# Hash bits of keys and queries from one four-column-group product set, and mask products over 32 rows

## The chip, the cores and the metric

The kernel runs on one core of one Trainium2 chip. The metric is device time in microseconds from the start to the end of one execution; several executions are timed and the median stands for the kernel. The engines are TensorE (PE; its weight loads are listed apart as PEld), VectorE (DVE), ScalarE (ACT), GpSimd (POOL) and SyncE (SP), which issues most DMAs. Each runs its own instructions in order and waits for the others by semaphores.

## What is computed

The reference is attention over 16 heads (2 batches of 8) of 768 tokens and 64 features, and behind it a gated layer and a layer of eight experts, which the change does not touch. What matters here is the mask of the attention: a query and a key see each other only when the signs of their six projections agree.

```
q_bits = (np.einsum('bhsd,dk->bhsk', q, proj) > 0).astype(np.int64)
k_bits = (np.einsum('bhsd,dk->bhsk', k, proj) > 0).astype(np.int64)
q_bucket = np.sum(q_bits * powers, axis=-1)
k_bucket = np.sum(k_bits * powers, axis=-1)
mask = q_bucket[:, :, :, None] == k_bucket[:, :, None, :]
scores = scale * np.matmul(q, k.transpose(0, 1, 3, 2))
scores = np.where(mask, scores, -1000000000.0)
attn = exp(scores - max); attn /= sum;  out = attn @ v
```

## The kernel before

**Pairs and units.** The 16 heads are taken as eight pairs. Of a pair i, the keys and queries are transposed by TensorE into `K[i]` and `Q[i]`: 64 features of one head in partitions 0 to 63, of the other in 64 to 127, with 768 tokens side by side. `QS` and `KS` are copies with the partition halves swapped, made by DMA. The attention runs over 48 units u, six for each pair; a unit is 256 queries of one head.

**Scores.** `scores(u, t)` with t = 0, 1 makes the scores of 128 queries against all 768 keys, in two PSUM banks of 384 keys (n = 0, 1). Two float32 products (line 270), one from the rows 0 to 63 and one from the rows 64 to 127, run side by side, each in two passes; then two bfloat16 products (line 273) add the mask to the same banks. For them `KF` holds the key's sign bits times 2^60, so that the maximum of a row is large only where all six bits agree, and a masked score vanishes in the exponential. The mask products read 64 rows at the same two places of the array as the score products; 7 bits of each head stand in 32 rows.

**Hash bits.** `lz` holds the projection as a weight block of 64 columns for a half. `signs(i, 0)` multiplies it with the two halves of `Q[i]` in two column groups of 64 (line 233), `signs(i, 1)` does so for `K[i]` (line 246). In the next unit ACT takes the signs of each (line 227, once for `QF`, once for `sk`), SP issues two DMAs that copy `QF` with its partition halves exchanged to `QG` (line 240), and `masks` multiplies `sk` twice into `KF` (line 216). `opening` does the same for the first pair, in smaller pieces.

**Order of the work.** The loop over u at the end of `attention` sets the order on every engine. On TensorE an iteration holds the scores (u + 1, 0), the scores (u + 1, 1), and then one of three things: half of the values' product `pv` of an earlier head (line 320, 96 passes on array tiles of 32 rows and 64 columns), or, in one of three iterations, a piece of a later pair: its transposes (`turned`, line 114) and its `signs` by turns, six iterations apart for each. DVE takes the row maxima (`nm`, line 278) and turns the exponentials in 32 by 32 blocks (`et`, line 308), ACT makes the exponentials (`e`, line 284) and copies `pv` out (lines 340), POOL normalises (line 301). The scores have two PSUM buffers of two banks, so the scores (u + 1, t) wait until the exponential of (u, t) has been read. `signs` and `turned` write the banks `pvb` that `pv` uses, so they wait for the copies on ACT, and the `pv` behind them waits for ACT to have read theirs. `hook` inserts pieces of weight conversion, and from unit 41 on the first products of the gated layer (line 597), at places fixed when the program is written.

Of the kernel before, what the change touches and what calls it, by code (L numbers as in the profile page):

```python
# [25 lines left out]
class Kernel:  # L26
# [8 lines left out]
    def constants(self, const):  # L35
        nc = self.nc
        NB, D = self.proj.shape[1], self.D
        self.ident = const.tile([128, 128], F32, name="ident")
        make_identity(nc, self.ident)

        p = const.tile([128, 2], I32, name="p")
        nc.gpsimd.iota(p[:, 0:1], pattern=[[0, 1]], base=0, channel_multiplier=1)
        nc.vector.tensor_scalar(p[:, 1:2], p[:, 0:1], 5, 1, ALU.logical_shift_right, ALU.bitwise_and)
        nc.vector.tensor_scalar(p[:, 0:1], p[:, 0:1], 31, None, ALU.bitwise_and)
        pf = const.tile([128, 2], F32, name="pf")
        nc.vector.tensor_copy(pf, p)
        bit = const.tile([128, 2], F32, name="bit")
        nc.vector.tensor_scalar(bit[:, 0:1], pf[:, 0:1], float(NB), None, ALU.is_lt)  # L50
        nc.vector.tensor_scalar(bit[:, 1:2], pf[:, 0:1], float(NB), None, ALU.is_equal)
        self.bias = const.tile([128, 1], F32, name="bias")
        nc.vector.scalar_tensor_tensor(self.bias, bit[:, 0:1], -1e-9, bit[:, 1:2], ALU.mult, ALU.add)
        fac = self.fac = const.tile([128, 2], F32, name="fac")
        nc.vector.tensor_scalar(fac[:, 0:1], bit[:, 1:2], -float(NB) * BIG, None, ALU.mult)
        nc.vector.scalar_tensor_tensor(fac[:, 0:1], bit[:, 0:1], BIG, fac[:, 0:1], ALU.mult, ALU.add)
        nc.vector.tensor_tensor(fac[:, 1:2], fac[:, 0:1], pf[:, 1:2], ALU.mult)
        nc.vector.tensor_tensor(fac[:, 0:1], fac[:, 0:1], fac[:, 1:2], ALU.subtract)
        self.lz = const.tile([128, 2, 2, 32], F32, name="lz")
        nc.gpsimd.memset(self.lz, 0.0)  # L60
        self.pr = const.tile([128, NB], F32, name="pr")
        const.tile([128, 72], F32, name="pad")

    def attention(self, xh, xl, pools, hook):
        nc = self.nc
        sb, ps_s, ps_pv = pools
        NB = self.proj.shape[1]
        S, D = self.S, self.D
        NC = S // 128
# [3 lines left out]
        H2 = S // 2  # L73
        for tag, shape, dt, n in (
            ("et", [128, NC * S], F32, 2), ("e", [128, 2 * S], F32, 3), ("vr", [128, NC * 256], F32, 2), ("raw", [128, 2 * S], F32, 1),
            ("q", [128, S], F32, 2), ("qs", [128, S], F32, 2), ("k", [128, S], F32, 2), ("ks", [128, H2], F32, 2),
            ("xp", [128, S], F32, 2), ("co", [128, S], F32, 2), ("qf", [128, H2], BF16, 2), ("qg", [128, H2], BF16, 2), ("kf", [128, S], BF16, 2), ("sk", [128, H2], BF16, 1),
        ):
            sb.tile(shape, dt, tag=tag, name=tag, bufs=n)
        raw, Q, QS, K, KS, QF, QG, KF, VR = {}, {}, {}, {}, {}, {}, {}, {}, {}  # L80

        def load(i, qs=(nc.sync, nc.sync)):
            b, hp = pairs[i]
# [15 lines left out]
        pvb = [ps_pv.tile([128, 2, 512], F32, tag=f"pv{n}", name="pv") for n in range(2)]  # L99
# [37 lines left out]
        def opening():  # L137
# [3 lines left out]
            lz = self.lz.rearrange("p a b c -> p (a b c)")  # L141
            for t, tag, n in ((Q, "q", S), (QS, "qs", S), (K, "k", S), (KS, "ks", H2)):
                t[0] = sb.tile([128, n], F32, tag=tag, name=tag, bufs=2)
            for t, tag in ((QF, "qf"), (QG, "qg")):
                t[0] = sb.tile([128, H2], BF16, tag=tag, name=tag, bufs=2)
# [19 lines left out]
            def sign(dst, src):  # L165
                nc.scalar.activation(dst, src, AF.Sign, bias=self.bias[:src.shape[0]], scale=2.0 ** 100)
# [15 lines left out]
            out(Q[0][:, queries], pvb[0][:, 1, :H2])  # L182
            for c in range(3, NC):
                first(pvb[1], 0, c)
            for x, r in enumerate(half):
                nc.tensor.matmul(
                    pvb[1][r, 0, :H2], lz[:, r], K[0][:, x * H2:(x + 1) * H2], start=True, stop=True, tile_position=(0, 64 * x)
                )
            sign(sk, pvb[1][:, 0, :H2])
            nc.tensor.matmul(pvb[0][:, 0, :H2], lz, Q[0][:, keys], start=True, stop=True)  # L190
            for x in range(2):
                sign((QF, QG)[x][0][half[x]], pvb[0][half[x], 0, :H2])
            for j in range(2):
                nc.vector.tensor_scalar(KF[0][:, j], sk, self.fac[:, j:j + 1], None, ALU.mult)
# [4 lines left out]
            def rest():  # L199
                nc.tensor.matmul(pvb[0][:, 1, :H2], lz, Q[0][:, queries], start=True, stop=True)  # L200

                def out(*_):
                    for x in range(2):
                        sign((QF, QG)[1 - x][0][half[x]], pvb[0][half[x], 1, :H2])

                return out

# [2 lines left out]
        later = []  # L210

        def masks(eng=nc.scalar):
            for kf, sk in later:
                for j in range(2):
                    if eng is nc.scalar:
                        eng.mul(kf[:, j], sk, self.fac[:, j:j + 1])
                    else:
                        eng.tensor_scalar(kf[:, j], sk, self.fac[:, j:j + 1], None, ALU.mult)
            later.clear()

        def signs(i, n):
            p = pvb[n]
            lz = self.lz.rearrange("p a b c -> p (a b c)")
            half = [slice(64 * x, 64 * x + 64) for x in range(2)]

            def sign(dst, src):
                nc.scalar.activation(dst, src, AF.Sign, bias=self.bias[:src.shape[0]], scale=2.0 ** 100)

            if n == 0:
                QF[i] = sb.tile([128, H2], BF16, tag="qf", name="qf", bufs=2)  # L230
                QG[i] = sb.tile([128, H2], BF16, tag="qg", name="qg", bufs=2)
                for x, r in enumerate(half):
                    nc.tensor.matmul(
                        p[r, 0, :H2], lz[:, r], Q[i][:, x * H2:(x + 1) * H2], start=True, stop=True, tile_position=(0, 64 * x)
                    )

                def out(*_):
                    sign(QF[i], p[:, 0, :H2])
                    for x in range(2):
                        nc.sync.dma_start(out=QG[i][half[1 - x]], in_=QF[i][half[x]])  # L240

                return out
            KF[i] = sb.tile([128, 2, H2], BF16, tag="kf", name="kf", bufs=2)
            sk = sb.tile([128, H2], BF16, tag="sk", name="sk", bufs=1)
            for x, r in enumerate(half):
                nc.tensor.matmul(
                    p[r, 0, :H2], lz[:, r], K[i][:, x * H2:(x + 1) * H2], start=True, stop=True, tile_position=(0, 64 * x)
                )

            def out(*_):  # L250
                sign(sk, p[:, 0, :H2])
                later.append((KF[i], sk))

            return out
# [7 lines left out]
        def scores(u, t):  # L262
            i, j, g = units[u]
            c = 2 * g + t
            st = ST[u, t] = ps_s.tile([128, 2, 512], F32, tag="s", name="st")
            ql = slice(c * 128, (c + 1) * 128)
            rows = [slice(64 * n, 64 * n + 64) for n in range(2)]
            for n, d in enumerate(rows):
                q, k = (Q[i], K[i][:, n * H2:(n + 1) * H2]) if n == j else (QS[i], KS[i])
                nc.tensor.matmul(st[:, n, :H2], q[d, ql], k[d], start=True, stop=False, tile_position=(64 * n, 0))  # L270
            for n, d in enumerate(rows):
                qf = (QF if n == c // (NC // 2) else QG)[i][d, c % (NC // 2) * 128:c % (NC // 2) * 128 + 128]
                nc.tensor.matmul(st[:, n, :H2], qf, KF[i][d, j], start=False, stop=True, tile_position=(64 * n, 0))  # L273

        def rowmax(u, t):
            if t == 0:
# [83 lines left out]
            nc.tensor.transpose(pvb[0][:, m % 2, m // 2 % 4 * 128:m // 2 % 4 * 128 + 128], self.ident, self.ident)  # L360
        for j in range(2):
            d = slice(64 * j, 64 * j + 64)
            for x in range(2):
                nc.vector.tensor_copy(self.lz[d, x, j, :NB], self.pr[d])
        rest = opening()
        load(1)
# [10 lines left out]
        for u in range(NU + 2):  # L377
# [33 lines left out]
            if u + 1 < NU:  # L411
                scores(u + 1, 1)
            if new < len(pairs):
                preps, held, held_kind = [kind(new, x) for x in ((1, 0) if kind is turned else (0, 1))], new, kind
            elif s != 1 and u >= 5:
                n = (u - 5) % 3
                pv((u - 5) // 3, range(12 * n, 12 * n + 12))
# [934 lines left out]
```

## Time and profile before

| | |
|---|---|
| median of 3 runs | 713.83 us (713.04 to 716.22) |
| profiled execution | 712.7 us |
| span of its instructions | 710.9 us |
| TensorE busy, attention to about 199 us, then the two layers | 693.8 us in all |
| matmul passes of line 270, line 273 | 384, 192 |
| matmul passes of line 233, line 246 | 28, 28 |

The 1.8 us between the span and the execution's own time lie around the instructions. The granted TensorE clock is 0.998, its upper level of 2.4 GHz, throughout. In the timeline a row gives start, duration, engine, line, operation, tiles, the array's rows*columns in use, and the shape of the moving operand. The duration of a pass reaches to the end of its modelled pipeline; the time for which it holds the array is the distance to the next pass on the same rows.

### The profile page before, as it was taken

Reading aid. Unit: us, or ns where it says so; the run is one execution under the profiler, and the core shown is the slowest. Engines: PE = TensorE matmul, PEld = TensorE weight load, DVE = VectorE, ACT = ScalarE, POOL = GpSimd, SP = SyncE. Lnnn points to the kernel's source line nnn. Section 1 sums busy time; section 2 is a strip of 40 time slices with the busy share of each in tenths; the row PEclk is TensorE's granted clock in tenths of the full one; section 3 lists DMA queues with packets and bytes.
Section 4 is the critical chain, followed back from the end, with each engine's and each line's share of the span. In section 5 each row is a group of like instructions: output and inputs, shape, how many; then the busy total and the mean of one; then the engine's idle time right before and its main releaser. Section 6 shows DMA issues by size and latency. Waiting matters only on the chain.

```text
span 710.9 us, 16289 instructions
## 1 busy us (share of the span) xinstructions
PE 693.8 (98%) x6796; PEld 583.5 (82%) x6796; DVE 453.6 (64%) x623; ACT 355.7 (50%) x660; POOL 435.4 (61%) x439
## 2 busy tenths in 40 slices
PE   8899999999999999999999999999999999999996
PEld 5465656566689999999999999988889899989995
DVE  4899999999966636546546456335646756556640
ACT  4789888988744341211212121234546565555560
POOL 1789999989964735636726537454525766657651
PEclk9999999999999999999999999999999999999999
DMA  6947754743241311211303201633533865676500
GB/s 151 211 106 182 162 126 116 171 114 96 47 136 60 120 61 60 67 52 60 119 0 108 71 12 48 234 108 104 169 110 101 284 229 197 205 258 226 208 37 24
DMA packets 68444, 88.00 MB, mean 124 GB/s; under 512 B 28931, under 2 KB 41027, under 8 KB 68368
## 3 DMA queue, kind: packets, MB, share of 16 engines
q1 hardware_dynamic: 63728, 78.41, 37.4%
q0 software_dynamic: 2560, 7.34, 2.7%
q10 hardware_dynamic: 2080, 1.18, 0.6%
q8 instruction: 54, 0.88, 0.5%
q14 instruction: 22, 0.18, 0.1%
HBM read 75.52 MB, written 7.34 MB: 117 GB/s over the span
## 4 chain that ended last, share of the span: by engine, by line
PE 82%; DVE 6%; ACT 5%; issue 3%; DMA 2%; POOL 2%; SPq 0%; POOLq 0%; ACTq 0%; DVEq 0%
PE ab L597 26%; PE yp L629 14%; PE op L974 11%; PE hp L924 10%; PE pv L320 8%; PE st L270 5%; DVE nm L278 3%; ACT e L284 2%; DVE et L308 2%; PE part L597 1%; PE st L273 1%; PE hr L942 1%; PE xgt L901 1%; ACT xp L340 1%; ACT co L340 1%
## 5 line engine op out<-in xcount | busy, mean ns | idle before, releaser
L597 PE MATMUL ab<-xh,w 128*128 128x384 f32 x704 | 185.7, 338 | 0.0
L597 PEld LDWEIGHTS ab<-xh,w 128*128 128x128 f32 x704 | 127.7, 188 | 2.0 <-issue 1.2
L597 PE MATMUL ab<-xl,w 128*128 128x384 f32 x352 | 118.3, 336 | 0.0
L612 POOL TENSOR_TENSOR g<-a,g 128x384 fp32r<-128x384 f32 x48 | 52.5, 1094 | 102.1 <-ACT g L611 101.9
L880 POOL TENSOR_TENSOR w<-raw,w 128x1024 fp32r<-128x1024 f32 x36 | 87.9, 2446 | 38.7 <-ACT w L879 37.2
L629 PE MATMUL yp<-w,g 128*128 128x512 f32 x432 | 102.9, 390 | 0.0
L301 POOL TENSOR_SCALAR e<-e,r,mc 128x768 f32<-128x768 f32 x96 | 93.7, 983 | 10.2 <-DVE r L288 10.0
L284 ACT ACTIVATE e<-st,nm 128x768 f32<-128x768 f32 x96 | 85.7, 896 | 27.4 <-DVE r L288 14.6
L278 DVE TENSOR_REDUCE nm<-st 128x1 f32<-128x768 f32 x96 | 90.0, 943 | 11.4 <-PE st L273 11.3
L629 PEld LDWEIGHTS yp<-w,g 128*128 128x128 f32 x432 | 80.4, 188 | 14.9
L270 PE MATMUL st<-k,q 64*128 64x384 f32 x192 | 83.4, 515 | 2.2 <-ACT e L284 1.9
L308 DVE STREAM_TRANSPOSE et<-e 128x1536 f32<-128x1536 f32 x48 | 84.8, 1768 | 0.0
L270 PE MATMUL st<-ks,qs 64*128 64x384 f32 x192 | 82.8, 511 | 1.9 <-ACT e L284 1.8
L974 PE MATMUL op<-w,hth 128*128 128x512 f32 x256 | 80.7, 396 | 0.0
L924 PE MATMUL hp<-xgh,w 128*128 128x256 f32 x448 | 80.7, 281 | 0.0
L611 ACT CAST g<-a 128x384 fp32r<-128x384 f32 x48 | 24.7, 515 | 111.5 <-DVE a L610 111.5
L320 PEld LDWEIGHTS pv<-et,vr 32*64 32x64 f32 x3072 | 60.2, 130 | 17.9 <-issue 8.7
L320 PE MATMUL pv<-et,vr 32*64 32x192 f32 x3072 | 72.5, 326 | 2.0 <-ACT q L128 1.6
L880 DVE TENSOR_TENSOR w<-raw,w 128x1024 fp32r<-128x1024 f32 x28 | 64.6, 2309 | 14.6 <-ACT w L879 14.6
L924 PEld LDWEIGHTS hp<-xgh,w 128*128 128x128 f32 x448 | 69.2, 188 | 0.3
L606 ACT COPY a<-ab 128x384 f32<-128x384 f32 x44 | 21.0, 476 | 95.1 <-PE ab L597 93.8
L597 PEld LDWEIGHTS ab<-xl,w 128*128 128x128 f32 x352 | 66.2, 188 | 0.8
(218 smaller groups left out, 1243.9 us busy)
## 6 DMA issues: line engine op xcount, KB each, us to landing
raw<-in_moe_w_dram SPq DMA_DIRECT2D x32, 1024.0 KB, 5.3
vr<-in_v_dram SPq DMA_DIRECT2D x64, 192.0 KB, 3.8
raw<-in_moe_w_a_dram SPq DMA_DIRECT2D x5, 1024.0 KB, 5.1
raw<-in_moe_w_b_dram SPq DMA_DIRECT2D x5, 1024.0 KB, 4.9
raw<-in_moe_w_out_dram SPq DMA_DIRECT2D x5, 1024.0 KB, 4.8
raw<-in_k_dram SPq DMA_DIRECT2D x16, 192.0 KB, 4.0
qs<-q SPq DMA_DIRECT2D x15, 192.0 KB, 3.8
raw<-in_q_dram SPq DMA_DIRECT2D x14, 192.0 KB, 4.1
```

The costliest lines, as they stand in the source:

```text
L270: nc.tensor.matmul(st[:, n, :H2], q[d, ql], k[d], start=True, stop=False, tile_position=(64 * n, 0))
L278: nc.vector.tensor_reduce(NM[u][:, t:t + 1], ST[u, t][:, :, :H2], axis=AX.XY, op=ALU.max, negate=True)
L284: nc.scalar.activation(halves(E[u][:, t]), ST.pop((u, t))[:, :, :H2], AF.Exp, bias=NM[u][:, t:t + 1], accum_out=SU[u][:, t:t + 1])
L301: nc.gpsimd.tensor_scalar(E[u][:, t], E[u][:, t], r[:, t:t + 1], c[:, t:t + 1], ALU.mult, ALU.add)
L308: nc.vector.transpose(ET[h][:, :, 2 * g:2 * g + 2].rearrange("p b c s -> p c b s"), E.pop(u).rearrange("p c (b s) -> p c b s", s=32),)
L320: nc.tensor.matmul(pvb[a // 2][m:m + 64, a % 2, :NC * 32], v[d], et[d, n].rearrange("p c s -> p (c s)"), start=(n < 2), stop=(n >= NB32 - ...
L597: nc.tensor.matmul(p[:, :384], w[:, k, fs], x[:, k, cols], start=(k == 0 and n == 0), stop=(k == self.KD - 1 and n == 2),)
L612: nc.gpsimd.tensor_tensor(gl[:, f], a, f32(gh[:, f]), ALU.subtract)
L629: nc.tensor.matmul(p, g[:, f, rows], w[:, f], start=(n == 0), stop=(n == 5))
L880: eng.tensor_tensor(l, raw, f32(h), ALU.subtract)
L924: nc.tensor.matmul(p[:, :256], w[:, k, fs], x[:, k], start=(n == 0), stop=(n == 3 * self.KD - 1))
L974: nc.tensor.matmul(p, h[:, 2 * n + f, rows], w[:, f], start=(n == 0 and f == 0 and m == 0), stop=(n == 3 and f == 1 and m == 2),)
```

## The change

`lz` becomes four column groups of 32, each with 16 columns for each head of a pair. `signs(i)` multiplies the two halves of the keys and the two halves of the queries in one set of four products, one per column group of 32 (line 225 of the new kernel), into one bank. ACT takes all signs with one instruction into `sk`. The keys' signs then lie in the rows 0 to 63 (32 for each half) and the queries' in 64 to 127. Four DMAs bring the queries' signs to `QF`, which now holds all 768 queries in the rows 0 to 31 and once more in 32 to 63; `QG` is gone. The two products of `masks` take 64 rows instead of 128. In `scores` the mask products read 32 rows at the array's rows 0 and 32, where they read 64 rows at 0 and 64 before. In `opening` each of the two steps that wrote parts of `QF` and `QG` becomes one. The constants of `fac` follow the new layout.

```diff
-            for n, d in enumerate(rows):
-                qf = (QF if n == c // (NC // 2) else QG)[i][d, c % (NC // 2) * 128:c % (NC // 2) * 128 + 128]
-                nc.tensor.matmul(st[:, n, :H2], qf, KF[i][d, j], start=False, stop=True, tile_position=(64 * n, 0))
+            for n in range(2):
+                d = slice(32 * n, 32 * n + 32)
+                nc.tensor.matmul(st[:, n, :H2], QF[i][d, ql], KF[i][d, j], start=False, stop=True, tile_position=(32 * n, 0))
...
-            for x, r in enumerate(half):
+            rows = [slice(32 * x, 32 * x + 32) for x in range(4)]
+            for x, r in enumerate(rows):
                 nc.tensor.matmul(
-                    p[r, 0, :H2], lz[:, r], K[i][:, x * H2:(x + 1) * H2], start=True, stop=True, tile_position=(0, 64 * x)
+                    p[r, 0, :H2], lz[:, r], (K, Q)[x // 2][i][:, x % 2 * H2:(x % 2 + 1) * H2],
+                    start=True, stop=True, tile_position=(0, 32 * x),
                 )
             def out(*_):
-                sign(sk, p[:, 0, :H2])
+                nc.scalar.activation(sk, p[:, 0, :H2], AF.Sign, bias=self.bias, scale=2.0 ** 100)
+                for y in range(2):
+                    for x in range(2):
+                        nc.sync.dma_start(out=QF[i][rows[y], x * H2:(x + 1) * H2], in_=sk[rows[2 + x]])
                 later.append((KF[i], sk))
...
-                    for x in range(2):
-                        sign((QF, QG)[1 - x][0][half[x]], pvb[0][half[x], 1, :H2])
+                    sign(QF[0][half[0], queries], pvb[0][half[0], 1, :H2])
...
-                preps, held, held_kind = [kind(new, x) for x in ((1, 0) if kind is turned else (0, 1))], new, kind
+                preps, held, held_kind = [turned(new, x) for x in (1, 0)] if kind is turned else [signs(new)], new, kind
```

On TensorE, in the iteration that makes the signs of a later pair, there stood before (x2 is two products in a row; the shape is that of the result, `st` the scores, `kf` and `qf`, `qg` the keys' and queries' bits):

```order
L270 MATMUL st<-k,q 128x384
L270 MATMUL st<-ks,qs 128x384
L273 LDWEIGHTS qg
L273 MATMUL st<-kf,qg 128x384
L273 LDWEIGHTS qf
L273 MATMUL st<-kf,qf 128x384
L233 MATMUL pv<-q,lz 64x384 x2
L246 MATMUL pv<-k,lz 64x384 x2
L270 MATMUL st<-ks,qs 128x384
```

and now:

```order
L253 MATMUL st<-k,q 128x384
L253 MATMUL st<-ks,qs 128x384
L256 LDWEIGHTS qf
L256 MATMUL st<-kf,qf 128x384
L256 LDWEIGHTS qf
L256 MATMUL st<-kf,qf 128x384
L225 MATMUL pv<-k,lz 32x384 x2
L225 MATMUL pv<-q,lz 32x384 x2
L253 MATMUL st<-ks,qs 128x384
```

Nothing changes its place on TensorE; the four sign products are of 32 result rows each, and both mask products load their weights from `qf`. On ACT, in the unit behind it, there stood before:

```order
L284 ACTIVATE e,su<-st,nm 128x768 x2
L227 ACTIVATE qf<-pv,bias 128x384
L227 ACTIVATE sk<-pv,bias 128x384
L216 ACTIVATE kf<-sk,fac 128x384 x2
L284 ACTIVATE e,su<-st,nm 128x768 x2
```

and now:

```order
L267 ACTIVATE e,su<-st,nm 128x768 x2
L231 ACTIVATE sk<-pv,bias 128x384
L214 ACTIVATE kf<-sk,fac 64x384 x2
L267 ACTIVATE e,su<-st,nm 128x768 x2
```

One instruction of seven such places is gone. On SP's queue, at the same place, before:

```order
L104 DMA qs<-q 64x768 x2
L94 DMA vr<-in_v_dram 32x4x384 x4
L240 DMA qg<-qf 64x384 x2
L94 DMA vr<-in_v_dram 32x4x384 x4
L87 DMA raw<-in_k_dram 128x6x64
```

and now:

```order
L104 DMA qs<-q 64x768 x2
L94 DMA vr<-in_v_dram 32x4x384 x4
L234 DMA qf<-sk 32x384 x4
L94 DMA vr<-in_v_dram 32x4x384 x4
L87 DMA raw<-in_k_dram 128x6x64
```

Four DMAs of half the size stand where two stood.

## Rows read from the trace of the kernel before

**Rows 1.** Busy time by engine in three stretches; PE, PEld, DVE, ACT, POOL, clock, DMA, GB/s.

```profile
80.50:103.80 23.30, 22.69 (x477) 14.43 (x477) 22.64 (x28) 20.41 (x43) 21.52 (x37) 1.00 0.69 155
174.50:198.50 24.00, 24.00 (x481) 16.69 (x480) 21.90 (x27) 17.45 (x37) 21.62 (x37) 1.00 0.29 68
400.00:420.00 20.00, 20.00 (x106) 18.59 (x105) 9.02 (x13) 4.35 (x8) 6.39 (x5) 1.00 0.16 53
```

**Rows 2.** Timeline of TensorE: scores of two halves of a unit, then `pv`.

```profile
85.68 0.32 PE L273 MATMUL st<-kf,qf 64*128 64x384 bf16 x1
...
85.84 0.48 PE L270 MATMUL st<-k,q 64*128 64x384 f32 x1
...
86.17 0.48 PE L270 MATMUL st<-k,q 64*128 64x384 f32 x1
...
86.50 0.32 PE L273 MATMUL st<-kf,qf 64*128 64x384 bf16 x1
86.75 0.42 PE L320 MATMUL pv<-et,vr 32*64 32x192 f32 x8
```

**Rows 3.** Timeline of TensorE where the array's rows or columns in use change.

```profile
12.92 0.32 PE L273 MATMUL st<-kf,qg 64*128 64x384 bf16 x1
13.17 0.59 PE L200 MATMUL pv<-q,lz 128*128 128x384 f32 x1
...
88.88 0.59 PE L270 MATMUL st<-k,q 64*128 64x384 f32 x1
...
89.31 0.48 PE L270 MATMUL st<-k,q 64*128 64x384 f32 x1
...
262.68 0.34 PE L597 MATMUL ab<-xl,w 128*128 128x384 f32 x1
262.86 0.34 PE L597 MATMUL ab<-xh,w 128*128 128x384 f32 x1
263.12 0.41 PE L662 MATMUL pe<-ident,emb 8*128 8x8 f32 x4
```

**Rows 4.** Timeline of the first masks: a weight load that nothing covers.

```profile
11.49 0.09 PEld L273 LDWEIGHTS <-qf 64*128 64x128 bf16 x1 [0.43 <-ACT qf L166]
...
11.51 0.32 PE L273 MATMUL st<-kf,qf 64*128 64x384 bf16 x1
...
12.10 0.33 PE L273 MATMUL st<-kf,qg 64*128 64x384 bf16 x1 [0.27 <-ACT qg L166]
```

**Rows 5.** Timeline of TensorE: column groups of 64, and later of 32.

```profile
91.04 0.87 PE L233 MATMUL pv<-q,lz 128*64 128x384 f32 x4 [0.27 <-ACT co L340]
91.74 0.81 PE L246 MATMUL pv<-k,lz 128*64 128x384 f32 x4
92.48 0.59 PE L270 MATMUL st<-ks,qs 64*128 64x384 f32 x1
...
475.92 0.85 PE L731 MATMUL lgt<-yt,enT 128*32 128x384 f32 x8
476.71 0.45 PE L597 MATMUL ab<-xh,w 128*128 128x384 f32 x1
```

**Rows 6.** Timeline of ACT beside the signs of a pair.

```profile
91.43 0.90 ACT L284 ACTIVATE e<-st,nm 128x768 f32<-128x768 f32 x1
92.23 0.20 ACT L284 ACTIVATION_READ_ACCUMULATOR e<-st,nm 128x1 f32 x1
```

**Rows 7.** Waits of TensorE: total us, times, longest.

```profile
PE st L270 <- ACT e L284: 3.7, 5, 1.4
PE pv L320 <- ACT q L128: 1.6, 5, 0.3
PE pv L233 <- ACT co L340: 1.5, 6, 0.3
```

**Rows 8.** Timeline of SP's issues and TensorE where the second pair's bits are first read.

```profile
29.73 1.11 SPq L240 DMA_DIRECT2D qg<-qf  x2
...
34.47 0.33 PE L273 MATMUL st<-kf,qg 64*128 64x384 bf16 x1 [0.97 <-DMA qg<-qf]
```

More of the change, by code (lines that the diff above doesn't have):

```diff
@@ L44, in constants @@
         nc.gpsimd.iota(p[:, 0:1], pattern=[[0, 1]], base=0, channel_multiplier=1)
-        nc.vector.tensor_scalar(p[:, 1:2], p[:, 0:1], 5, 1, ALU.logical_shift_right, ALU.bitwise_and)
-        nc.vector.tensor_scalar(p[:, 0:1], p[:, 0:1], 31, None, ALU.bitwise_and)
+        nc.vector.tensor_scalar(p[:, 1:2], p[:, 0:1], 4, 1, ALU.logical_shift_right, ALU.bitwise_and)
+        nc.vector.tensor_scalar(p[:, 0:1], p[:, 0:1], 15, None, ALU.bitwise_and)
         pf = const.tile([128, 2], F32, name="pf")
@@ L58, in constants @@
         nc.vector.tensor_tensor(fac[:, 0:1], fac[:, 0:1], fac[:, 1:2], ALU.subtract)
-        self.lz = const.tile([128, 2, 2, 32], F32, name="lz")
+        self.lz = const.tile([128, 4, 2, 16], F32, name="lz")
         nc.gpsimd.memset(self.lz, 0.0)
@@ L76, in attention @@
             ("q", [128, S], F32, 2), ("qs", [128, S], F32, 2), ("k", [128, S], F32, 2), ("ks", [128, H2], F32, 2),
-            ("xp", [128, S], F32, 2), ("co", [128, S], F32, 2), ("qf", [128, H2], BF16, 2), ("qg", [128, H2], BF16, 2), ("kf", [128, S], BF16, 2), ("sk", [128, H2], BF16, 1),
+            ("xp", [128, S], F32, 2), ("co", [128, S], F32, 2), ("qf", [128, S], BF16, 2), ("kf", [128, S], BF16, 2), ("sk", [128, H2], BF16, 1),
         ):
             sb.tile(shape, dt, tag=tag, name=tag, bufs=n)
-        raw, Q, QS, K, KS, QF, QG, KF, VR = {}, {}, {}, {}, {}, {}, {}, {}, {}
+        raw, Q, QS, K, KS, QF, KF, VR = {}, {}, {}, {}, {}, {}, {}, {}
         def load(i, qs=(nc.sync, nc.sync)):
@@ L143, in opening @@
                 t[0] = sb.tile([128, n], F32, tag=tag, name=tag, bufs=2)
-            for t, tag in ((QF, "qf"), (QG, "qg")):
-                t[0] = sb.tile([128, H2], BF16, tag=tag, name=tag, bufs=2)
+            QF[0] = sb.tile([128, S], BF16, tag="qf", name="qf", bufs=2)
             KF[0] = sb.tile([128, 2, H2], BF16, tag="kf", name="kf", bufs=2)
@@ L184, in opening @@
                 first(pvb[1], 0, c)
-            for x, r in enumerate(half):
+            for x in range(2):
+                r = slice(32 * x, 32 * x + 32)
                 nc.tensor.matmul(
-                    pvb[1][r, 0, :H2], lz[:, r], K[0][:, x * H2:(x + 1) * H2], start=True, stop=True, tile_position=(0, 64 * x)
+                    pvb[1][r, 0, :H2], lz[:, r], K[0][:, x * H2:(x + 1) * H2], start=True, stop=True, tile_position=(0, 32 * x)
                 )
-            sign(sk, pvb[1][:, 0, :H2])
+            sign(sk[half[0]], pvb[1][half[0], 0, :H2])
             nc.tensor.matmul(pvb[0][:, 0, :H2], lz, Q[0][:, keys], start=True, stop=True)
-            for x in range(2):
-                sign((QF, QG)[x][0][half[x]], pvb[0][half[x], 0, :H2])
+            sign(QF[0][half[0], keys], pvb[0][half[0], 0, :H2])
             for j in range(2):
-                nc.vector.tensor_scalar(KF[0][:, j], sk, self.fac[:, j:j + 1], None, ALU.mult)
+                nc.vector.tensor_scalar(KF[0][half[0], j], sk[half[0]], self.fac[half[0], j:j + 1], None, ALU.mult)
             out(QS[0][half[1], queries], pvb[1][half[1], 1, :H2])
@@ L202, in out @@
                 def out(*_):
-                    for x in range(2):
-                        sign((QF, QG)[1 - x][0][half[x]], pvb[0][half[x], 1, :H2])
+                    sign(QF[0][half[0], queries], pvb[0][half[0], 1, :H2])
                 return out
@@ L212, in masks, with signs @@
         def masks(eng=nc.scalar):
+            d = slice(0, 64)
             for kf, sk in later:
                 for j in range(2):
[L215 to L218, printed above, removed]
+                    eng.mul(kf[d, j], sk[d], self.fac[d, j:j + 1])
             later.clear()
-        def signs(i, n):
-            p = pvb[n]
+        def signs(i):
+            p = pvb[0]
@@ L223, in signs @@
             lz = self.lz.rearrange("p a b c -> p (a b c)")
[L224 to L242, printed above, removed]
+            QF[i] = sb.tile([128, S], BF16, tag="qf", name="qf", bufs=2)
@@ L243, in signs @@
             KF[i] = sb.tile([128, 2, H2], BF16, tag="kf", name="kf", bufs=2)
             sk = sb.tile([128, H2], BF16, tag="sk", name="sk", bufs=1)
-            for x, r in enumerate(half):
+            rows = [slice(32 * x, 32 * x + 32) for x in range(4)]
+            for x, r in enumerate(rows):
                 nc.tensor.matmul(
-                    p[r, 0, :H2], lz[:, r], K[i][:, x * H2:(x + 1) * H2], start=True, stop=True, tile_position=(0, 64 * x)
+                    p[r, 0, :H2], lz[:, r], (K, Q)[x // 2][i][:, x % 2 * H2:(x % 2 + 1) * H2],
+                    start=True, stop=True, tile_position=(0, 32 * x),
@@ L248, in signs @@
                 )
             def out(*_):
-                sign(sk, p[:, 0, :H2])
+                nc.scalar.activation(sk, p[:, 0, :H2], AF.Sign, bias=self.bias, scale=2.0 ** 100)
+                for y in range(2):
+                    for x in range(2):
+                        nc.sync.dma_start(out=QF[i][rows[y], x * H2:(x + 1) * H2], in_=sk[rows[2 + x]])
                 later.append((KF[i], sk))
@@ L362, in attention @@
             d = slice(64 * j, 64 * j + 64)
-            for x in range(2):
+            for x in range(4):
                 nc.vector.tensor_copy(self.lz[d, x, j, :NB], self.pr[d])
```

## The prediction

> **What bounds the kernel now.** I read the busy time by stretches first. From 220 us on TensorE has no gap (20.00 us busy of 20.00 in the stretch from 400 us [rows 1]) and the change touches nothing there, so what counts is when TensorE gets through the attention. There it is close to full, and DVE is too: 22.69 and 22.64 us busy of 23.30 in a cycle of six units in the middle, 24.00 and 21.90 of 24.00 in the last six [rows 1]. So a unit has two limits that nearly touch. The waits of TensorE [rows 7] tell which one ends last: in the whole program 3.7 us for the exponentials (5 times, up to 1.4 us, in the first units), 1.6 us where `pv` waits for ACT to have read a pair's transposes, and 1.5 us where the signs' products wait for ACT's copies. Elsewhere in the attention TensorE runs on without a wait. It is the bound from unit 7 on, with eleven places where ACT holds it for 0.3 us at most.
>
> The timeline of one unit shows what a mask product costs now. The first starts at 85.68, the score pass behind it on the same rows at 85.84: 0.16 us, and no gap between the two, though one is float32 and the other bfloat16 [rows 2]. A score pass takes 0.33 us (85.84 to 86.17), and the weights of all that follows on the same array shape load behind running products.
>
> Where the shape changes it is otherwise. The last mask starts at 86.50 and holds the array to 86.66; `pv`, on tiles of 32 by 64, starts at 86.75 [rows 2]. A mask that starts at 12.92 ends at 13.08; a product on 128 rows and the same 128 columns starts at 13.17. A pass of line 597 that starts at 262.86 lasts until 263.04 (such passes are 0.18 us apart) and the product of 8 rows and 128 columns behind it starts at 263.12 [rows 3]. In each case 0.08 to 0.09 us pass without a product. Then the weights must load with nothing to cover them: after a change to 64 rows the first score pass starts at 88.88 and the second at 89.31, 0.43 us apart and not 0.33: 0.10 to 0.11 us of uncovered float32 load [rows 3]. A bfloat16 load is cheap: where the first mask had waited for ACT its load starts at 11.49 and the product at 11.51, 0.02 us later [rows 4].
>
> **The change part by part.** *Masks on 32 rows.* Score products stay on 64 rows by 128 columns, masks go to 32 by 128. That is a change of shape in the middle of every one of the 96 calls of `scores`: 0.09 us of gap and 0.02 us of load, 0.11 us. Between the scores (u, 0) and (u, 1), which follow each other directly, the array must also change back: 0.09 and 0.11, 0.20 us. Behind (u, 1) another shape comes in any case, and that change is paid already. A unit thus costs TensorE 2 x 0.11 + 0.20 = 0.42 us more. The mask products themselves stay at 0.16 us: the moving operand still has 384 columns, and the two still lie on different rows.
>
> No row shows a change from 64 to 32 rows with the same 128 columns; the nearest are those from 64 to 128 rows and from 128 to 8 [rows 3], and I take their price. The Trainium skill, TensorEngine Tiling (Array Packing), section Key Properties, says that a change of the tiling mode, not merely of the tile, drains the array, and lists 64 by 128 and 32 by 128 as two modes. It speaks against this change: by it the time would be that of the sum below, 724.9. The bounds of the load of a mask are 0 and the 0.11 us of a float32 load [rows 3]; I take 0.02, since that row is of the same load with more rows. A unit is then between 0.38 and 0.60 us.
>
> *Where that counts.* From unit 7 to unit 47 there are 41 units, 17.2 us. Not all of it moves the end. Around the signs of a pair ACT ends last: the last mask before them ends at 86.66 and the next scores start at 92.48 [rows 2, 5], 5.82 us later, and the exponential they wait for is read out at 92.43 (92.23 + 0.20) [rows 6]. TensorE's own work in this interval becomes 2.22 (`pv` and its changes, 86.66 to 88.88) + 1.03 and 1.12 (the two score calls: 0.11 + 0.65 + 0.11 + 0.16, and 0.20 + 0.65 + 0.11 + 0.16) + 0.79 (gap, load and two passes of signs) + 0.09 = 5.25 us. It stays below ACT's 5.77, so the interval keeps its length: the unit's 0.42 us is hidden, and what the signs save is lost with it. Where `pv` waits for a pair's transposes the wait of 0.3 us [rows 7] and a smaller one of the scores before it take up about the unit's 0.42 as well. Six pairs have their signs after unit 7 and five their transposes: 11 of 41 units are free, and 30 x 0.42 = 12.6 us remain. In the first cycles DVE still holds some units, as its 22.64 us of 23.30 let expect [rows 1]; I take off 1.0 us (0 to 2).
>
> *The signs.* Two sets of two column groups take 91.04 to 92.48, 1.44 us; a set of four groups of 32 takes 0.79 us in the same kernel (eight passes, 475.92 to 476.71) [rows 5]. So a pair saves 0.65 us on TensorE, and ACT one instruction of 0.6 us, behind which only its own queue waits. By the paragraph above both fall into time that ACT's copies and exponentials set, and I count them at nothing (down to -0.65 x 6 = -3.9 us if ACT, too, ran earlier). The two products of `masks` take fewer partitions and the same 384 columns: no change.
>
> *The DMAs.* Four issues in place of two; SP takes 1.11 us for two [rows 8], so 1.1 us more in its queue, in front of the loads of `vr` and `raw`, which are used units later. Only the second pair reads its bits as soon as they land: TensorE waits there 0.97 us until 34.47 [rows 8]. The second product's bits now come with the third DMA and not the first: 0 to 1.1 us later, I take 0.6. From the third pair on the signs are read three units after they are made (made at 91 us for a pair whose scores begin at 103.8, the start of the next cycle), long after a landing.
>
> *The opening.* The first scores wait for two sign instructions on ACT, 11.51 and 12.10 [rows 4]; one is gone, 0.6 us earlier. Then the first seven units, which run from exponential to scores and back, each carry the 0.11 us of a mask on that path. I set the two against each other: 0 (-0.6 to +0.7).
>
> **Sum:** 12.6 - 1.0 + 0.6 + 0 = 12.2 us. On the profiled execution's 712.7 us that is 724.9. The median of the three runs lies 1.1 us above the profiled one; I forecast 725.0. With each unknown at its ends: 0.38 a unit, 2 us taken off, the opening's gain and no later DMA give 30 x 0.38 - 2.0 - 0.6 = 8.8, so 721.5; 0.60 a unit gives 30 x 0.60 = 18.0, 2 us more where the free units no longer hide it, and 1.1 for the DMA: about 733.
>
> **The rivals.** *First, not slower: splitting a 64-row tile is no change of shape.* The array's lower 64 rows may take two tiles of 32 without coming to rest, and the masks' weights may load under the running score pass, as they do now under a pass on their own rows. The Trainium skill, TensorE: Matmul & The Clock Gate, section Part 3, says that weight loads pass running products where their row groups differ, which would cover the loads for the two masks in part. For it speaks the missing gap between scores and masks now [rows 2]; against it, every change of the row count that the trace has, 64 to 128 and 128 to 8, costs the gap [rows 3]. Then nothing is added but the DMA (+0.6) and the opening gains up to 0.6; the signs give 0 to -3.9: 709 to 713.5, likeliest 712.5, no change.
>
> *Second: only one way costs.* The masks slip in behind the score pass, the way back pays 0.20 us: 30 x 0.20 is 6.0, less the 1.0: about 718.
>
> *Third: masks' loads cost like float32.* 0.60 a unit as above, about 731.5. Against it the 0.02 us of [rows 4].
>
> *Fourth: the change does not do what it says,* and the four column groups follow each other: four products of 0.65 us, one behind the other, where now two pairs of them take 1.3, so 1.3 us a pair more than now, of which the 0.52 us between 5.25 and 5.77 hide only part; with the masks' price about 733. Against it the set of four in 0.79 us [rows 5].
>
> **How the numbers follow.** The forecast's mechanism has 0.73, the first rival 0.12, the second 0.05, the third 0.06, the fourth 0.04. The range reaches from 717.0, which takes in the second rival, to 731.5; it leaves out the first rival and half of the third and fourth, less than 0.2 with the tails. A difference of 0.5%, 3.6 us, is about what a measurement of this kernel can tell from no change: slower by more holds the forecast, third, fourth and half of the second, 0.85; within it lies the rest of the second and most of the first, 0.12; faster by more 0.03.
>
> **What the profile after would show.** Between the last score pass of a call and its first mask a gap of 0.11 us more than the pass, and 0.20 us before the scores (u, 1); a call pair that takes 2.1 and not 1.7 us; a cycle of six units of about 24.8 us and not 23.3; no waits of `pv` on ACT and none of the signs' products; DVE's busy share in the attention down by some 6%; the four sign products within 0.03 us of each other; from 225 us on the same distances as before. The prediction is wrong if the masks start 0.33 us after the second score pass with no gap, or if the waits on ACT grow instead of vanishing.

## The result and the profile after

The changed kernel takes 724.46 us (median of 4 runs, 723.35 to 728.12), the kernel before in runs on the same chip 714.99 us (4 runs, 713.04 to 716.22): a ratio of 1.0144, with a 95% interval from 1.0098 to 1.019. The forecast was 725.0. By the medians the change costs 9.5 us, where 725.0 on the 713.83 us known before meant 11.2. The profiled execution took 724.84 us with a span of 722.9 us, 12.0 us more than the span before. The forecast's sum of 12.2 us was made on that profiled execution before.

On the page the chain that ended last shows where the time went. Its first line gives the shares by engine, of before and then of after:

```profile
PE 82%; DVE 6%; ACT 5%; issue 3%; DMA 2%; POOL 2%; SPq 0%; POOLq 0%; ACTq 0%; DVEq 0%
```

```profile
PE 86%; ACT 4%; issue 3%; DVE 3%; DMA 2%; POOL 1%; SPq 0%; POOLq 0%; ACTq 0%; DVEq 0%
```

TensorE has taken 4% of the span from DVE, ACT and POOL. The busy time of the changed kernel in the middle cycle, from the scores of unit 18 to those of unit 24, with the columns of [rows 1]:

```profile
83.05:107.75 24.70, 24.18 (x477) 13.62 (x476) 23.07 (x28) 20.28 (x42) 21.51 (x36) 1.00 0.64 148
```

It is the cycle that took 23.30 us before [rows 1], with the same 477 matmuls and the same 28 instructions on DVE; it now takes 24.70. TensorE's busy share is 98% where it was 97%: a gap of 0.1 us behind a modelled end doesn't show as idle time, so the share hides the loss, and the same count in a longer stretch shows it. DVE goes from 97% to 93%. The granted clock is at its upper level.

TensorE's timeline of one unit shows the gaps (start, duration, line, result<-operands, rows*columns of the array, moving operand):

```profile
87.42 0.59 PE L253 MATMUL st<-k,q 64*128 64x384 f32 x1
...
87.84 0.48 PE L253 MATMUL st<-k,q 64*128 64x384 f32 x1
...
88.26 0.09 PEld L256 LDWEIGHTS <-qf 32*128 32x128 bf16 x2 [0.55 <-issue]
88.26 0.34 PE L256 MATMUL st<-kf,qf 32*128 32x384 bf16 x2
88.53 0.59 PE L253 MATMUL st<-k,q 64*128 64x384 f32 x1
...
88.95 0.48 PE L253 MATMUL st<-k,q 64*128 64x384 f32 x1
...
89.38 0.34 PE L256 MATMUL st<-kf,qf 32*128 32x384 bf16 x2
89.64 2.21 PE L303 MATMUL pv<-et,vr 32*64 32x192 f32 x96
```

From the second score pass to the mask it is 0.42 us (87.84 to 88.26) where the pass holds the array for 0.33: 0.10 us more than before [rows 2]. From the mask's start to the next scores it is 0.27 where it was 0.16, and the next score pass follows after 0.42 and not 0.33: 0.20 us on the way back. The two calls of `scores` of a unit take 2.12 us, from 87.42 to the end of the last mask (89.38 and 0.16). Of the 96 changes from 64 rows to 32 in the trace, all but the one that waits for a DMA show the same distance to 0.01 us, 0.41 to 0.42. The masks' loads start at 88.26, with the first mask and not under the score pass; in the kernel before, such a load ran under the second score pass:

```profile
86.17 0.09 PEld L273 LDWEIGHTS <-qg 64*128 64x128 bf16 x1
```

The waits of TensorE (total us, times, longest):

```profile
PE st L253 <- ACT e L267: 6.3, 11, 1.0
PE pv L343 <- POOL ident masks.py:199: 1.3, 1, 1.3
PE pv L152 <- DMA raw<-in_k_dram: 0.9, 1, 0.9
PE pv L303 <- issue: 0.8, 1, 0.8
PE st L256 <- DMA qf<-sk: 0.6, 1, 0.6
```

The waits of `pv` and of the signs' products on ACT [rows 7] are gone. Those of the scores for the exponentials have grown from 5 to 11; five of 0.52 us each lie behind the signs of a pair, two of 0.24 and 0.27 us at 45.6 and 50.3 us.

### The profile page after: what moved, and what is told of

Read it like the earlier page. It is cut to its first block, busy times and chain, and to the rows that moved or that the text cites. A ratio compares the mean times of both kernels' runs of the same rounds, so it can differ in the third digit from the quotient of the medians.

```text
span 722.9 us, 16280 instructions
## 1 busy us (share of the span) xinstructions
PE 706.0 (98%) x6796; PEld 577.5 (80%) x6796; DVE 455.1 (63%) x627; ACT 355.2 (49%) x651; POOL 436.1 (60%) x439
## 4 chain that ended last, share of the span: by engine, by line
PE 86%; ACT 4%; issue 3%; DVE 3%; DMA 2%; POOL 1%; SPq 0%; POOLq 0%; ACTq 0%; DVEq 0%
PE ab L580 24%; PE yp L612 13%; PE op L957 10%; PE hp L907 10%; PE pv L303 9%; PE st L253 9%; PE st L256 3%; ACT e L267 1%; PE part L580 1%; PE pv L580 1%; PE pv L114 1%; PE hr L925 1%; PE xgt L884 1%; DMA raw<-in_k_dram 1%; ACT co L323 1%
## 5 line engine op out<-in xcount | busy, mean ns | idle before, releaser
L595 POOL TENSOR_TENSOR g<-a,g 128x384 fp32r<-128x384 f32 x48 | 55.7, 1161 | 103.0 <-ACT g L594 103.0
L261 DVE TENSOR_REDUCE nm<-st 128x1 f32<-128x768 f32 x96 | 91.5, 954 | 19.2 <-PE st L256 15.9
L253 PE MATMUL st<-ks,qs 64*128 64x384 f32 x192 | 87.2, 534 | 5.0 <-ACT e L267 5.0
L253 PE MATMUL st<-k,q 64*128 64x384 f32 x192 | 87.3, 535 | 1.4 <-ACT e L267 1.2
L594 ACT CAST g<-a 128x384 fp32r<-128x384 f32 x48 | 24.8, 516 | 109.9 <-DVE a L593 109.9
L617 DVE TENSOR_TENSOR y<-yp,y 128x512 f32<-128x512 f32 x60 | 41.5, 692 | 39.5 <-PE yp L612 39.4
```

The costliest lines, as they stand in the source:

```text
L261: nc.vector.tensor_reduce(NM[u][:, t:t + 1], ST[u, t][:, :, :H2], axis=AX.XY, op=ALU.max, negate=True)
L595: nc.gpsimd.tensor_tensor(gl[:, f], a, f32(gh[:, f]), ALU.subtract)
```

## The experiments

All kernels compute the whole reference. The times of the first four stand beside a median of 712.95 us of the kernel before, those of the other four beside 712.78 us.

**Masks on 32 rows alone** (signs, DMAs and ACT as before; of the 64 rows of a half the 32 with the unit's head are read):

```diff
-            for n, d in enumerate(rows):
+            for n in range(2):
+                r = 64 * n + 32 * j
+                d = slice(r, r + 32)
...
-                nc.tensor.matmul(st[:, n, :H2], qf, KF[i][d, j], start=False, stop=True, tile_position=(64 * n, 0))
+                nc.tensor.matmul(st[:, n, :H2], qf, KF[i][d, j], start=False, stop=True, tile_position=(r, 0))
```

> The kernel before with one part of the change alone: the mask products read 32 rows (the 32 of their head, at the array's rows 0 and 64 or 32 and 96), while signs, QF, QG and DMAs stay. Theory (the change of the array's shape inside every call of scores costs, the rest of the change does not matter): about 12 us slower than before, 724 to 727, and 0 to 1 us slower than the whole change, since the signs' two sets now fill the time that ACT sets: the masks start 0.10 us later than the end of the second score pass, and 0.10 us and a load of 0.11 pass before the scores (u, 1). Rival (the mask rows cost nothing, the slowdown comes from the signs, their DMAs or the new layout): like before, 713 to 716.

Measured: 724.96 us (724.49 to 726.46), ratio 1.0175 (1.0158 to 1.0192). This part alone makes the whole slowdown. Its timeline has the distances of the changed kernel to 0.01 us (0.42, 0.26, 0.43):

```profile
88.60 0.48 PE L270 MATMUL st<-k,q 64*128 64x384 f32 x1
...
89.02 0.33 PE L275 MATMUL st<-kf,qf 32*128 32x384 bf16 x1
...
89.28 0.59 PE L270 MATMUL st<-k,q 64*128 64x384 f32 x1
...
89.71 0.48 PE L270 MATMUL st<-k,q 64*128 64x384 f32 x1
```

The two masks here lie at the rows 0 and 64 (32 and 96 for the other head) and in the changed kernel at 0 and 32: the price comes with the size of the tile and not with its place. That settles the first rival (no change of shape, 712.5) and the second (only one way costs, 718): both ways cost.

**Signs alone** (four column groups, one ACT instruction, four DMAs; the masks stay on 64 rows, for which `fac` is zero in the rows of the other operand; for that the kernel makes two small constants more at its start, and its opening takes the signs on all 128 rows):

```diff
-                    p[r, 0, :H2], lz[:, r], (K, Q)[x // 2][i][:, x % 2 * H2:(x % 2 + 1) * H2],
+                    p[r, 0, :H2], lz[:, r], (K, Q, Q, K)[x][i][:, x // 2 * H2:(x // 2 + 1) * H2],
...
-                        nc.sync.dma_start(out=QF[i][rows[y], x * H2:(x + 1) * H2], in_=sk[rows[2 + x]])
+                        r = 32 + 32 * x - 32 * y
+                        nc.sync.dma_start(out=QF[i][64 * y:64 * y + 64, x * H2:(x + 1) * H2], in_=sk[r:r + 64])
```

(against the changed kernel)

> The changed kernel with the masks' products back on 64 rows: one set of four column groups in the order keys, queries, queries, keys, one sign instruction, four DMAs of 64 rows into QF, KF zero in the middle rows. Theory: no change of shape between scores and masks, so like before within 2 us (712 to 716); the 0.65 us a pair that the signs save on TensorE stay hidden behind ACT, the interval from the last mask before a pair's signs to the next scores stays at 5.8 us. Rival A (signs or DMAs cost): 720 or more. Rival B (the saving counts): 3 to 4 us faster than before, and that interval 0.65 us shorter.

Measured: 716.79 us (716.29 to 719.27), ratio 1.0062 (1.0038 to 1.0085): slower than before, and 0.8 us above the highest that was expected. In the attention the cost is a single event. Against the kernel before, the scores of unit 7 start 3.31 us late, and from there to the last scores the distance stays between 2.6 and 3.3 us. Another 1.6 us come behind the last scores, almost all in the layers, in steps of a few nanoseconds (below). The event begins on SP's queue:

```profile
22.79 3.67 SPq L96 DMA_DIRECT2D raw<-in_q_dram  x1
...
31.26 2.41 SPq L243 DMA_DIRECT2D qf<-sk  x4
```

One issue of a load holds SP for 3.67 us, where the longest of these issues before took 1.25. The bits' DMAs are issued at 31.26, behind it in the queue, and not at 29.73 [rows 8]. TensorE then waits, and what follows runs slower:

```profile
35.81 0.44 PE L264 MATMUL st<-kf,qf 64*128 64x384 bf16 x1 [3.01 <-DMA qf<-sk]
36.46 0.50 PE L264 MATMUL st<-kf,qf 64*128 64x384 bf16 x1 [0.21 <-DMA qf<-sk]
...
37.26 0.84 PE L262 MATMUL st<-k,q 64*128 64x384 f32 x1
```

A pass of 0.48 us takes 0.84 here. The busy time of the stretch from 34 to 40 us gives the granted clock, 0.72 on the mean, where the same stretch of the kernel before has 1.00; passes at this distance are those of the lower level, 1.2 GHz:

```profile
34.00:40.00 6.00, 3.99 (x64) 2.41 (x72) 2.43 (x4) 2.00 (x5) 1.87 (x2) 0.72 1.10 218
```

The signs of the later pairs, each 0.65 us shorter on TensorE, save nothing: from 50 us to the last scores the distance to the kernel before changes for good at one place alone, by 0.4 us, and the kernel before with only its loads exchanged (below) gains the same 0.4 there. It is a half of `pv` that takes 2.57 us to the next scores in the kernel before (110.00 to 112.57), where the usual one takes 2.13 [rows 2, 3], with no wait on another engine recorded:

```profile
110.00 2.64 PE L320 MATMUL pv<-et,vr 32*64 32x192 f32 x96
```

**Masks first** in the second call of a unit, so that two pairs of masks stand side by side (changed kernel otherwise; `products` issues the score products of a call, `bits` its masks):

```diff
+            for x, step in enumerate((products, bits) if t == 0 else (bits, products)):
+                step(x == 0)
```

> The changed kernel, but in the scores (u, 1) the mask products come first and the score products second, so that from (u, 0) to (u, 1) the masks of both stand together and a unit has two changes of shape of its own and not three. Theory (each change is a fixed price): a unit loses one entry of 0.10 us, some 30 units of 41 show it: 2.5 to 4 us faster than the whole change, about 721 (8 to 9.5 us slower than before). Rival (the price is one of the 32-row tiles themselves, for instance their slower products, and not of the changes): the same as the whole change within 1 us.

Measured: 720.53 us (719.87 to 722.14), ratio 1.0112 (1.0095 to 1.013), 4.4 us less than the masks alone in the same comparison and 7.6 above the kernel before, a little under the 8 to 9.5 expected:

```profile
87.31 0.48 PE L254 MATMUL st<-k,q 64*128 64x384 f32 x1
...
87.73 0.50 PE L259 MATMUL st<-kf,qf 32*128 32x384 bf16 x4
88.16 0.59 PE L254 MATMUL st<-k,q 64*128 64x384 f32 x1
88.17 0.59 PE L254 MATMUL st<-ks,qs 64*128 64x384 f32 x1
88.59 0.48 PE L254 MATMUL st<-k,q 64*128 64x384 f32 x1
```

The four masks run as one group without a gap (87.73 to 88.16 is two passes of about 0.16 and one gap), and of the three changes a unit two are left. A unit whose `pv` stands between costs 0.31 us more than before (4.26 us from one `pv` to the next), not 0.41. The cost goes with the number of changes; the work is the same.

**The sign set twice** (the second writes the same values again):

```diff
-            for x, r in enumerate(rows):
+            for _ in range(2):
+                for x, r in enumerate(rows):
```

> The changed kernel with the set of four sign products issued twice in a row into the same place, so that TensorE spends 0.65 us more for each of seven pairs. Theory (ACT sets the interval around the signs, and TensorE has 0.5 to 0.6 us to spare there): the wait of the next scores for the exponential, 0.59 us in the changed kernel, goes to zero and the interval grows by 0.1 us at most, 0 to 1 us in all. Rival (TensorE's time counts everywhere): 4.5 us slower than the whole change.

Measured: 723.32 us (723.05 to 727.67), ratio 1.0166 (1.0132 to 1.0199): no difference from the changed kernel that can be told. First the changed kernel, then this one, where the signs stand between two units:

```profile
94.00 0.52 PE L225 MATMUL pv<-k,lz 128*32 128x384 f32 x2
94.02 0.52 PE L225 MATMUL pv<-q,lz 128*32 128x384 f32 x2
...
94.36 0.49 PE L225 MATMUL pv<-q,lz 128*32 128x384 f32 x2
95.37 0.59 PE L253 MATMUL st<-ks,qs 64*128 64x384 f32 x1 [0.52 <-ACT e L267]
```

```profile
94.11 0.52 PE L226 MATMUL pv<-k,lz 128*32 128x384 f32 x2
...
94.78 0.49 PE L226 MATMUL pv<-k,lz 128*32 128x384 f32 x2
...
95.11 0.49 PE L226 MATMUL pv<-k,lz 128*32 128x384 f32 x2
...
95.54 0.59 PE L254 MATMUL st<-ks,qs 64*128 64x384 f32 x1
```

The wait of 0.52 us for the exponential is filled by the second set and gone. From the end of the last mask before the `pv` (89.38 + 0.16 = 89.54) to these scores it is 5.83 us in the changed kernel and 5.89 with twice the signs (from 89.65), against 5.82 before [rows 2, 5]. A sign set is free there, and so is what was saved of it.

**Signs alone, with the loads of `vr` moved behind the bits' DMAs** at the second pair; and the same exchange in the kernel before:

```diff
             preps = []
+            if u == 4:
+                load_v(1)
...
-            if s == 0 and u >= 3 and u // 3 < 2 * len(pairs):
+            if s == 0 and u > 3 and u // 3 < 2 * len(pairs):
```

> The kernel e2_signs_only with the loads of the second head's values issued behind the four DMAs of the second pair's bits and not before them. In e2_signs_only TensorE waited 3.0 us for these bits and then ran its next products at half clock; the kernel was 2.6 us behind the one before at the end of the attention and 4 us in all. Theory (that one late landing is the loss, the signs themselves cost and save nothing): the wait falls below 1 us, the clock stays up, 712 to 714.5. Rival (the signs in four column groups or the wider DMAs cost something in every pair): still 715 to 717.

> The kernel before with the same exchange of two loads in SP's queue: its wait of 0.97 us for the second pair's bits goes, and up to 1 us with it: 712 to 713.5, no difference that can be told from before. It is the control of e5_signs_bits_first: the two should be equal within 1 us if the four column groups are worth nothing here; 3 to 4 us apart (e5 faster) if each pair's 0.65 us counted.

Measured: signs alone 715.37 us (714.19 to 715.87), ratio 1.0037 (1.0022 to 1.0052), 0.9 us above the highest that was expected; the kernel before 713.0 us (712.19 to 714.35), ratio 1.0002 (0.9987 to 1.0018). The first time lies in the rival's range (715 to 717), and 2.4 us above the control where at most 1 was expected. In both the wait for the bits is gone, and the first keeps the full clock in the attention: the late bits were the event above. The load that held SP for 3.67 us there takes 2.03 here, so the exchange is not all that differs. But neither keeps the gain. Signs alone stands 1.60 us ahead of the kernel before at unit 7, 0.62 ahead at 133 us and 1.00 behind it at the last scores, where the control stands 0.80 behind: there the two are 0.2 us apart. Of what the first loses, 0.80 goes in a `pv` at 133 us and 0.77 at 163 us, where the scores wait 1.35 us for the exponential and not 0.58. In the kernel before the 0.61 us gained at unit 7 go in two places, in the middle of a `pv`, where no wait on another engine is recorded:

```profile
41.47 0.88 PE L320 MATMUL pv<-et,vr 32*64 32x192 f32 x24 [0.74 <-issue]
...
135.73 0.87 PE L320 MATMUL pv<-et,vr 32*64 32x192 f32 x22 [0.49 <-issue]
```

The changed kernel has one such pause (0.8 us, below); the kernel before has none that long, but two slow halves of `pv` (2.56 us from 39.49, and the one at 110.00 above). What makes them, and whether an earlier start brings them about, stays open. So does a further loss of 1.3 us behind the last scores of the first of the two, most of it in the layers in steps under 0.08 us, where its control loses nothing. The signs alone above has the same drift: in both, the distances between products of `yp` add up to 0.90 us more than before. The changed kernel and the one with the signs twice have the same four column groups and no such drift, so it comes with what these two kernels have besides them; no run says with what. What the pair shows is that inside the attention the signs alone buy nothing, even where their queue is mended.

**Masks on 32 rows in one call of two**, the second or the first of a unit, with the diff of the first experiment and

```diff
+                r, m = (64 * n + 32 * j, 32) if t == 1 else (64 * n, 64)
```

(`t == 0` in the other). If changes of shape are what costs, the second call alone pays only the way in, 0.10 us, since `pv` behind it changes the shape in any case; the first pays the way in and back, 0.30.

> The kernel e1_masks32_only with the 32-row masks in the scores (u, 1) alone; the scores (u, 0) keep 64 rows. Theory (a price for each change of shape): only the entry of 0.10 us a unit is new, since another shape follows (u, 1) in any case: 2.5 to 4 us slower than before, 715.5 to 717. Rival (32-row masks cost by themselves, half of them half of the price): 6 us slower, about 719.

> The other half: 32-row masks in the scores (u, 0) alone. Theory: entry of 0.10 us and way back of 0.10 us with an uncovered load of 0.11 us, 0.31 us a unit: 8 to 9.5 us slower than before, 721 to 722.5; with e7_masks32_t1 about the 12 us of e1_masks32_only. Rival: 6 us slower, about 719, the same as e7_masks32_t1.

Measured: the second call 714.77 us (713.95 to 716.06), ratio 1.0026 (1.0013 to 1.0039); the first 719.67 us (718.86 to 720.26), ratio 1.0105 (1.0088 to 1.0122). Both lie below what was expected. The first call's time comes close to the rival's 719, but the rival asked for two equal times, and they are 4.9 us apart. Second call alone, then first call alone:

```profile
85.96 0.32 PE L275 MATMUL st<-kf,qf 64*128 64x384 bf16 x1
...
86.12 0.48 PE L270 MATMUL st<-k,q 64*128 64x384 f32 x1
...
86.44 0.48 PE L270 MATMUL st<-k,q 64*128 64x384 f32 x1
...
86.86 0.33 PE L275 MATMUL st<-kf,qg 32*128 32x384 bf16 x1
```

```profile
86.59 0.33 PE L275 MATMUL st<-kf,qf 32*128 32x384 bf16 x1
...
86.85 0.59 PE L270 MATMUL st<-k,q 64*128 64x384 f32 x1
...
87.28 0.48 PE L270 MATMUL st<-k,q 64*128 64x384 f32 x1
87.60 0.32 PE L275 MATMUL st<-kf,qg 64*128 64x384 bf16 x1
```

Where nothing else holds TensorE the prices are as the theory has them: a unit with `pv` takes 3.95 us before, 4.06 with the second call alone, 4.26 with the first alone, 4.36 with both. The totals don't add up in the same way, 2.0 and 6.9 us against 12.0 for both: a span with signs or transposes and one full unit grows by 0.4 us with both, by 0.2 with the first alone and by 0 to 0.1 with the second alone. TensorE has some time to spare there (the waits of `pv` and the signs on ACT, 0.3 us each [rows 7]), and each kernel alone uses it before it costs anything, which both together can do only once. My expectations counted that too low. The profiled execution of the second call alone was the slowest of its eight (716.06 us) and has a span 3.3 us longer than before; 1.7 of these came at 132 to 146 us, in two slow halves of `pv` like those above (3.13 and 2.69 us in place of 2.13).

## Why the prediction was right, and where its sizes were off

**The bound.** TensorE was the bound and became more so: its chain share rose, DVE's busy share in the middle cycle fell from 97% to 93% (some 4%, where I had said 6%), and a cycle of six units takes 24.7 us where I had 24.8. Right.

**The price of a change.** I took 0.11 us for the way in and 0.20 for the way back from changes to other row counts [rows 3], 0.42 a unit. Measured are 0.10, 0.20 and 0.10: 0.41 between one `pv` and the next, 3.95 to 4.36. The 0.20 are a gap of 0.10 and an uncovered float32 load of 0.10. Right to 0.01. What the Trainium skill, TensorEngine Tiling (Array Packing), section Key Properties, says of drains at a change of the tiling mode agrees with these kernels: the 0.09 to 0.10 us stand at each change of shape, and between products of one shape, as in the calls with masks of 64 rows, there is no gap. The price itself is this trace's.

**The units that are free.** The interval around the signs kept its length as worked out, 5.83 us against 5.82, with the predicted wait of the scores for ACT (0.52, I had 5.77 - 5.25), and twice the signs showed the same. The waits of `pv` around the transposes vanished as well. I had named growing waits on ACT as a sign of being wrong: the scores' grew by 2.6 us, behind the signs as forecast, but all waits on ACT of [rows 7] together went from 6.8 to 6.3. I took off 1.0 us for units that DVE held, and what came off was 1.8. In the eleven spans that hold signs or transposes, from the second of one `pv` pair to the first of the next, the distance grew by 2.71 us, where one full unit each makes 11 x 0.41 = 4.5. Some of these spans were longer before than the usual 7.61 us (7.93 at 39 us, 7.89 at 75, 8.00 at 110). At 75 us it was a wait of the scores for the exponential, time that TensorE had to spare and has now used. At 39 and 110 us it was the two slow halves of `pv`, 0.43 us each, which take the usual 2.13 in the changed kernel: half of the 1.8 is thus not shown to be DVE's, and its cause stays open. The 1.8 lay inside my bounds of 0 to 2, but only in part for my reason. From unit 7 to the end of the attention the change costs 10.5 us, and I had 11.6.

**The opening and the DMA.** One sign instruction less starts unit 1 0.38 us earlier, and the mask on each early unit's path eats that by unit 6 (0.01 us ahead): 0, as forecast. The bits of the second pair come as worked out:

```profile
29.72 2.48 SPq L234 DMA_DIRECT2D qf<-sk  x4
```

Four issues take 2.48 us where two took 1.11 [rows 8], and the first mask of the pair starts at 34.03 and not 33.18, 0.85 us later. But the second mask had waited 0.97 us before [rows 8] and comes with the first now, so that unit 7 starts only 0.22 us late, its predecessor's own changes of shape included, where I counted 0.6 for the DMA.

**The layers.** Here I was wrong: I had the same distances from 225 us on. The changed kernel loses 1.3 us behind the last scores, 0.56 up to the first product of `yp` and 0.73 later:

```profile
216.72 1.19 PE L303 MATMUL pv<-et,vr 32*64 32x192 f32 x37 [0.83 <-issue]
...
251.61 1.30 PE L612 MATMUL yp<-w,g 128*128 128x512 f32 x5
253.21 2.11 PE L612 MATMUL yp<-w,g 128*128 128x512 f32 x8 [0.31 <-POOL g L595]
```

```profile
251.06 2.10 POOL L595 TENSOR_TENSOR g<-a,g 128x384 fp32r<-128x384 f32 x1 [2.36 <-ACT g L594]
```

The first is a pause inside the last `pv`, of the kind seen above. The second is a POOL instruction of 2.10 us, which takes 1.02 at this place in the kernel with the masks alone and 1.01 in the one with the signs twice; TensorE waits for it, 0.6 us with the load that follows uncovered. Such a long run of it is nothing new: the kernel before has three (the first is shown below) and the masks alone six, but there TensorE doesn't wait.

```profile
312.58 2.10 POOL L612 TENSOR_TENSOR g<-a,g 128x384 fp32r<-128x384 f32 x1 [6.84 <-ACT g L611]
```

Neither the masks alone nor the signs twice, which have the same changes of shape, lose anything behind the last scores, so neither event belongs to the shapes. The sum thus came out at 12.0 by three terms that were off: 10.5 (I had 11.6), 0.2 (0.6) and 1.3 (0). The mechanism was right; part of the close total is luck. Luck is also in the base: the four executions before spread from 713.04 to 716.22 us, and against 714.99 the cost is 9.5 us.

Two sums of the bounds were loose. The upper end, 18.0 + 2 + 1.1 = 21.1 us on 712.7, is 733.8 and not about 733; and the second rival's 718 counts from the profiled execution, the third's 731.5 from the median. Neither touches the forecast.

**The signs.** A set takes 0.69 us (94.00 to 94.69, a pass of 0.33 behind 94.36) and 0.10 behind it (95.11 to 95.54 with the set twice, less the pass), 0.79 in place of 1.44, as I had it, and its four products start within 0.02 us of each other, so the fourth rival fell. Counting the saving at nothing was right: signs alone brought no gain, and a second set cost nothing that can be told. Two ways in which the signs' DMAs could cost more (a full queue in front of the bits, a clock at half behind the wait) were not in the prediction; they did not strike the changed kernel but did strike the signs alone.

No kernel of these was faster than the one before.

## What to carry over

Count the changes of the array's shape that an edit adds to TensorE's order, each at its measured gap and the weight load that loses its cover (here 0.10 us for a bfloat16 load and 0.20 for a float32 load), before counting what it saves in rows or columns: here fewer rows saved no time at all. Products of one shape belong side by side; where a narrower operand must stand between wider ones, as the masks here, padding it to their rows was cheaper. And work taken off TensorE between two units buys nothing where another engine's chain sets when the next unit may start.

## What was not expected of the hardware

The changed kernel shows 0.10 us behind a mask of 32 rows and 0.09 behind a product of 64 rows, but the number of rows is not shown to be the reason. With the masks first, the second of two such masks is followed by the scores after 0.25 us and not 0.26, while it starts 0.17 us behind the first and not 0.16: that points to the first mask behind a change as the place of the 0.01.

One DMA issue held SP for 3.67 us, nearly three times as long as any of the same loads before, in a kernel that starts them 0.6 us earlier. It moved everything queued behind it; why it took so long isn't shown.

After 3.01 us without work, TensorE's passes took 0.84 us in place of 0.48 for 3.4 us, at the lower level of its granted clock (0.72 on the mean of the six microseconds from 34 us). A wait of three microseconds cost more than itself.
